# Retention and MLP on one core: one group of units fewer turned on TensorE, another order of loads, other rules of joining visits

## The chip, the cores and the metric

The kernel runs on one core of one Trainium2 chip. The time is the device time of one execution in microseconds; the median of several executions is given.

## The reference

The inputs are q, k and v of 8 batches x 8 heads x 576 positions x 64, and two weights of an MLP, 512 x 2048 and 2048 x 512, all fp32.

```python
scores = scale * np.matmul(q, k.transpose(0, 1, 3, 2))
gamma = 1.0 - 2.0 ** (-5.0 - np.arange(H, dtype=np.float32))
rel = pos[:, None] - pos[None, :]
Dmat = np.where(rel >= 0, gamma[:, None, None] ** rel[None, :, :], 0.0)
attn_out = np.matmul(scores * Dmat[None, :, :, :], v)
...
x = np.ascontiguousarray(attn_out.transpose(0, 2, 1, 3)).reshape(B * S, H * D)
h = x @ w_in
g = 0.5 * h * (1.0 + erf(h * inv_sqrt2))
out = g @ w_out
```

So it is a causal attention with a decay in place of the softmax, and behind it an MLP with an exact GELU over 4608 tokens.

## The kernel before

**Units and groups.** The attention is cut into 36 units of 128 tokens with all 8 heads: for each pair of batches `bp` and chunk of positions `ci`, one unit for each batch `j`; the last chunk has 64 positions and holds both batches in one unit. Units 0 to 3 are the first chunks of batches 0 to 3 and are groups 0 to 3; after them a group is the two units of one `(bp, ci)`, so group 4 is units 4 and 5, group 5 units 6 and 7. There are 22 groups. Because the decay is a power, a chunk needs only its own keys (a masked product) and a state `u` of the chunks before it. Four units make a block of 512 tokens, x of that block, and the MLP runs over 9 blocks.

**Stages of a group.** Loads go through POOL's DMA queue and cast fp32 to bf16 on the way. `T`: q and k are turned (positions to the free axis). For groups 0 to 3 and for the `NPE` groups from 4 on (`BY_PE`) this is `turn`: 8 matmuls against an identity for q and 8 for k (line 528 calls the helper on line 454), and a copy out of PSUM by DVE or ACT, whichever is free sooner (`either`, lines 485 and 487). For the others (`BY_DVE`) it is `turn_dve`: q and k are loaded in another layout (line 346, runs of four positions), DVE transposes 32 x 32 blocks (line 548), and ACT takes q apart (`apart`, line 559). `S`: scores on TensorE, then the mask on DVE (line 612 or 617). `vh`: values scaled by the decay, on ACT, DVE or POOL (lines 634 and 638). `A`, a visit (`attend`): the products of scores and values, the new state, the product of q with the old state, and x out of PSUM by DVE (lines 785 and 789). `AA` is one visit for two groups. The state needs the keys in natural layout: for `BY_PE` groups that is the tile k was loaded in, for `BY_DVE` groups an extra tile `kn`, loaded by line 352.

**MLP.** The first product with w_in (`mlp1`, and `mlp1_fast` for the last three blocks), GELU on ACT, and the second product with w_out (`mlp2` for half of block 0, `mlp2_fast` for the rest). The fast forms use seven products in place of eight with sums made on DVE. `wi0` to `wi7` and `wo0` to `wo7` are 256 KB pieces of the two weights (lines 310 and 325), each needed by a part of the columns. `mlp1` of block 0 can start on a piece of w_in and one unit of x; `mlp2` of block 0 takes the pieces of w_out in order.

**What sets the order.** The instruction lists are written when the kernel is built, by a planner that keeps a clock for each engine (`T`), an estimate for each instruction and landing times for the loads. At each step it emits what its clock calls ready: attention first (A, U for a state, S, T), otherwise a step of the MLP. On the chip each engine then runs its list in order and waits on semaphores. A load is emitted from the list `ORDER` whenever POOL's clock is within 1.5 us of TensorE's; `q5` means q of unit 5, `n6` the keys of units 6 and 7 in natural layout, `io` and `dq` are small computations on POOL. Item `n` of a `BY_PE` group does nothing (line 329). After the list, later groups are loaded as buffers come free. While TensorE has nothing to do early on, the planner emits products of zeros (`warm`).

The constants in the diff are read in these lines:

```python
tied = 4 <= n < N_G - 1 and units[g[0]][1] == units[groups[n + 1][0]][1] and n >= VISIT and nB - 4 * b1 > LEAD
...
hold = both <= now + NEAR
...
if n < nT and n not in [x[0] for x in apart_due] and g[-1] // 4 <= tM1 + N_XB - 1 and nA + len(g) <= AHEAD + early + RATE * b1:
    return sg[n]["T"]
...
if T["dve"] <= now + (SB + JOIN_SB if after_a else SB) and nA - nB <= 2:
    acts.append((max(s_ready(JOIN if after_a else 0), fetch_at(64 if n >= 4 else 0), free_time(0, len(g))), "S"))
```

`nB` counts units attended, `nA` units whose scores are made, `b1` blocks through the first MLP product. A tied group waits for its partner if the partner is ready within `NEAR`. `SLACK`, `PER_G`, `PER_B` and `TURN0` rank DVE's side jobs, `SEM` is the planner's time for a semaphore, `STATE10` the earliest time of one state, and `MSK_AT` the time from which DVE may build the mask for groups 4 and later (`make_msk`, lines 213 and 215).

Of the kernel before, what the change touches and what calls it, by code (L numbers as in the profile page):

```python
# [17 lines left out]
def kernel(  # L18
# [48 lines left out]
    pair_of = {key: [units.index((*key, 0)), units.index((*key, 1))] for key in {x[:2] for x in units if x[2] is not None}}  # L67

    PLAIN = 4
    NPE = 2  # L70
    FAST1 = (5, 6, 7, 8)[PLAIN // 4:]
    FAST2 = tuple(range(1, N_BLK))
    BY_PE = range(4, 4 + NPE)
    BY_DVE = range(4 + NPE, N_G)
    raw = range(4)
# [6 lines left out]
    N_VH = 4  # L82
    VH_ACT = [4, 22, 1]
    N_XB = 4
    AHEAD = 35
    RATE = 0.4
    STORE_AT = 62.0
    CROWD = 66.0
    STATE10 = 28.0
    HOT = 8.0  # L90
    FETCH = 5.0
    ARRIVE = 5.4
    WARM_TO = 24.0
    JOIN = 1
    JOIN_SB = 0.0
    VISIT = 8
    LEAD = -3.0
    NEAR = 3.2
    SLACK, SB, PER_G, PER_B, TURN0 = 1.2, 2.0, 8.0, 20.0, 0.0
    FINE = 0.38  # L100
    FPOOL = 0.6
    N_V = 6
    N_WARM = 10
    MSK_AT = -58.0
    HK = N_DF // 2

    const = ctx.enter_context(tc.tile_pool(name="const", bufs=1))
# [11 lines left out]
    mode = ["full"]  # L119
    DRAIN = 0.25  # L120
    port_end = [0.0]
    SEM = 0.12
    OVER = {"dve": 0.06}

    pool_runs = []
# [96 lines left out]

    later = [(7.3, "act", 1.4, warm_gelu), (MSK_AT, "dve", 0.8, make_msk)]
    T["act"], T["dve"], T["pool"] = 2.6, 2.9, 1.25
# [39 lines left out]
    def all_loaded():  # L264
        return not ORDER and next_load[0] >= N_G

# [38 lines left out]
    def load(what, i):  # L305
# [56 lines left out]
        for jj in (j,) if j is not None else range(2):  # L362
# [3 lines left out]
            else:  # L366
# [6 lines left out]
    land["v", 0] = 6.2  # L373
    cast_due = {("q", 0): (loaded[0][0][0], first["q32"]), ("k", 0): (loaded[0][0][1], first["k32"])}
    cast_due["v", 0] = (loaded[0][1], first["first_v"])
    ORDER = ("wi4 io wo2 q2 q1 k1 k2 wi5 wi3 n4 v1 wi1 v2 wi0 wi2 k3 q3 v3 wi7 dq2 wi6 wo6 q4 wo4 q5 wo0 wo1 wo3 "
             "wo5 k5 wo7 q6 k4 k7 v4 q7 k6 q8 v6 q12 dq0 q9 v12 k9 k13 q10 n8 k11 k8 v8 dq3 k10 q11 v10 k12 n10 "
             "dq4 q13 n6 n12").split()

    def next_order():  # L380
        item = ORDER.pop(0)
        what = item.rstrip("0123456789")
        load(what, int(item[len(what):] or 0))
# [5 lines left out]
    def reload():  # L389
        if next_load[0] < N_G:  # L390
            g = groups[next_load[0]]
            ORDER.extend([f"{what}{i}" for what in "qk" for i in g] + [f"{what}{g[0]}" for what in ("vn" if len(g) > 1 else "v")])
            next_load[0] += 1
# [46 lines left out]
    def release(b, when):  # L440
        held.remove(b)
        free_at[b] = when
# [72 lines left out]
    def turn(n, jj):  # L515
# [15 lines left out]
        release(b, done + 0.05)  # L531
        sg[n]["T"] = max(sg[n].get("T", 0.0), done + SEM)

# [7 lines left out]
    def turn_dve(n, x):  # L541
# [6 lines left out]
        nc.vector.transpose(dst.rearrange("p (h b t) -> p h t b", h=HP, b=32), src)  # L548
        done = on("dve", 0.13 + m / 530, max(land["qk"[x], i] for i in groups[n])) + SEM
        if x == 0:  # L550
# [4 lines left out]
    def apart():  # L555
# [4 lines left out]
                       sg[n]["pairs"].rearrange("p h s -> p (h s)")[:, 0:2 * m].rearrange("p (n y) -> p y n", y=2))  # L560
        sg[n]["T"] = max(sg[n].get("T", 0.0), on("act", 0.15 + m / 580, ready) + SEM)

# [38 lines left out]
    def masked(i):  # L601
# [8 lines left out]
        if i in raw:  # L610
            for e in range(2):
                nc.vector.tensor_tensor(both[:, HP * e:HP * e + HP, :], t[:, e], near[e], op=ALU.mult)
                s["R"] = on("dve", 0.66, done) + SEM
                release(two[e], s["R"])
            return
        by = (msk2 if short else msk).unsqueeze(1).to_broadcast([128, 2, HP, w])
        nc.vector.tensor_tensor(both.rearrange("p (e h) s -> p e h s", e=2), t, by, op=ALU.mult)  # L617
        s["R"] = on("dve", 0.15 + H * w / 960, done) + SEM
        for b in two:
# [6 lines left out]
    def scaled_v(n, engine):  # L626
# [5 lines left out]
        if engine == "act":  # L632
            for h in range(H):
                nc.scalar.activation(vh[:, 0:m, h], src[:, :, h], AF.Copy, scale=dv[:, h, ci:ci + 1])  # L634
            done = on("act", 1.65 + 0.4 * m, ready) + SEM
        else:
# [7 lines left out]
    def out_pairs(n):  # L644
        return 2 if n >= 4 else 0
# [566 lines left out]
    def fire():  # L1212
        now = T["pe"]
        while ORDER and T["pool"] <= now + 1.5:
            next_order()
# [47 lines left out]
    def attend(*ns):  # L1263
        nonlocal nB
        two = out_banks(ns) if ns[0] >= 4 else ()
        for i in [i for n in ns for i in groups[n]]:
            inner(i)
            nB += 1
        while u_due and state_at(*u_due[0]) <= T["pe"] + 0.2 and not (u_due[0] == (1, 0) and T["pe"] <= STATE10):
            state(*u_due[0])  # L1270
# [13 lines left out]
    def s_ready(early=0):  # L1284
        n = group_of[nA]
        g = groups[n]
        if n < nT and n not in [x[0] for x in apart_due] and g[-1] // 4 <= tM1 + N_XB - 1 and nA + len(g) <= AHEAD + early + RATE * b1:
            return sg[n]["T"]
# [14 lines left out]
    while True:  # L1303
# [18 lines left out]
        if nB < nA:  # L1322
# [3 lines left out]
            ready = ready_for(n)  # L1326
            tied = 4 <= n < N_G - 1 and units[g[0]][1] == units[groups[n + 1][0]][1] and n >= VISIT and nB - 4 * b1 > LEAD
            if tied:
                both = 1e9
                if nA > groups[n + 1][-1] and one_piece(384 if len(g) > 1 else 192):  # L1330
                    both = max(ready, ready_for(n + 1))
                    acts.append((max(both, fetch_at(384 if len(g) > 1 else 192), free_time(len(g) > 1 and units[g[0]][1] < NCI - 1, out_pairs(n))), "AA"))
                hold = both <= now + NEAR
                alone = max(ready, free_time(n < 4, out_pairs(n)))
            else:
                acts.append((max(ready, fetch_at(192 if n >= 4 else 0), free_time(n < 4, out_pairs(n))), "A"))
        for key in u_due[:1]:
            if key != (1, 0) or now > STATE10:
                acts.append((state_at(*key), "U"))
        if nA < N_U:  # L1340
            n = group_of[nA]
            g = groups[n]
            if T["dve"] <= now + (SB + JOIN_SB if after_a else SB) and nA - nB <= 2:
                acts.append((max(s_ready(JOIN if after_a else 0), fetch_at(64 if n >= 4 else 0), free_time(0, len(g))), "S"))
        if nT < 4 + NPE and nT <= group_of[min(nA, N_U - 1)] + 3 and (nT < 4 or not half or ring_free("tk")):
            keys = [("qk"[half], i) for i in groups[nT]]
# [102 lines left out]
```

## Time and profile before

| | us |
|---|---|
| median of 3 runs (lowest, highest) | 288.04 (287.86, 289.65) |
| the profiled execution | 288.46 |
| its span, first to last instruction | 286.7 |
| TensorE busy in the span | 277.8 (97%) |
| DVE, ACT, POOL busy | 229.7, 176.7, 141.0 |
| moved by DMA | 31.97 MB |

The profile is of one execution. Its lines name an engine, the line of the kernel, the operation and its tiles (out<-in), how many and how long. TensorE's matmuls overlap one another, so a run of them is longer than the distance to the next start, and distances between starts are the better measure. Line 450 is the helper that records all matmuls, line 454 the one for transposes.

### The profile page before, as it was taken

The numbers are of one execution on the slowest core, as the hardware profiler recorded it, in microseconds if no ns is written. First come the engines' busy times: TensorE is split into PE (matmuls) and PEld (weight loads), VectorE is DVE, ScalarE is ACT, GpSimd is POOL, SyncE is SP. The second block draws the span as 40 slices with busy tenths as digits, with TensorE's granted clock in tenths as the row PEclk, the third lists the DMA queues.
The fourth block names the chain that finished last, engine by engine and source line by source line (L and its number), as shares of the span: only waits on it lengthen the run. The fifth ranks groups of instructions, "written<-read, shape, count | busy, mean of one in ns | idle before, by whom it ended". The sixth has DMA issues, their size and how long they took to land.

```text
span 286.7 us, 9851 instructions
## 1 busy us (share of the span) xinstructions
PE 277.8 (97%) x4216; PEld 210.3 (73%) x4216; DVE 229.7 (80%) x387; ACT 176.7 (62%) x403; POOL 141.0 (49%) x213
## 2 busy tenths in 40 slices
PE   7889998999999999999999999999999999999994
PEld 2568766888864657756676676677888888888883
DVE  6754586767995699898978599969999999999861
ACT  7456425876888895688587766764555363655421
POOL 8976898799959977778665864000000000000000
PEclk9999999999999999999999999999999999999999
DMA  9999999999999999999999996302020201202014
GB/s 158 176 179 188 195 152 173 188 132 143 128 154 108 116 167 120 205 146 135 142 150 160 101 139 54 71 2 75 2 75 0 77 4 72 75 0 75 37 57 129
DMA packets 109276, 31.97 MB, mean 112 GB/s; under 512 B 85936, under 2 KB 104880, under 8 KB 109232
## 3 DMA queue, kind: packets, MB, share of 16 engines
q0 software_dynamic: 100528, 21.12, 83.8%
q1 hardware_dynamic: 6752, 9.37, 9.9%
q10 hardware_dynamic: 1952, 0.85, 1.3%
q8 instruction: 33, 0.54, 0.8%
q14 instruction: 11, 0.09, 0.1%
HBM read 42.99 MB, written 9.44 MB: 183 GB/s over the span
## 4 chain that ended last, share of the span: by engine, by line
PE 61%; DMA 22%; POOL 12%; issue 2%; ACT 1%; DVE 0%; POOLq 0%
PE psum L450 60%; DMA kn_ld<-in_k_dram 6%; DMA w_out<-in_moe_w_out_dram 6%; DMA q_ld<-in_q_dram 5%; POOL k_ld L346 3%; POOL q_ld L346 2%; DMA v_ld<-in_v_dram 2%; DMA early<-in_q_dram 2%; POOL v_ld L357 2%; DMA k_ld<-in_k_dram 1%; POOL dqT L320 1%; PE psum L454 1%; POOL kn_ld L352 1%; POOL w_in L310 1%; POOL k_ld L336 1%
## 5 line engine op out<-in xcount | busy, mean ns | idle before, releaser
L450 PE MATMUL psum<-x,w_in 128*128 128x256 bf16 (+2 forms) x792 | 117.8, 295 | 0.6 <-DMA w_in<-in_moe_w_in_dram 0.6
L450 PEld LDWEIGHTS <-w_in 128*128 128x128 bf16 x792 | 69.0, 98 | 29.1 <-DMA w_in<-in_moe_w_in_dram 1.2
L450 PEld LDWEIGHTS <-g_all 128*128 128x128 bf16 x576 | 55.5, 98 | 13.5 <-issue 0.3
L450 PE MATMUL psum<-w_out,g_all 128*128 128x256 bf16 (+1 forms) x440 | 57.9, 280 | 0.0
L346 POOL DMA_DIRECT2D k_ld<-in_k_dram x64 | 35.5, 577 | 23.8 <-DMA kn_ld<-in_k_dram 14.1
L816 ACT ACTIVATE g_all<-psum 128x512 bf16<-128x512 f32 x64 | 36.9, 592 | 16.4 <-PE psum L450 14.8
L450 PEld LDWEIGHTS <-s 128*128 128x128 bf16 x408 | 39.5, 98 | 7.6 <-issue 0.6
L634 ACT ACTIVATE vh<-v_ld,dv 128x128 bf16<-128x128 bf16 (+1 forms) x144 | 42.1, 378 | 0.0
L617 DVE TENSOR_TENSOR ret<-psum,msk 128x1024 bf16<-128x1024 f32 (+1 forms) x32 | 35.5, 1149 | 6.3 <-PE psum L450 6.2
L1030 ACT ACTIVATE g_all<-t 128x512 bf16<-128x512 f32 x36 | 22.6, 630 | 28.2 <-DVE t L1038 28.2
L487 ACT COPY t<-psum 128x256 f32<-128x256 f32 (+1 forms) x48 | 20.7, 433 | 29.7 <-PE psum L450 29.5
L346 POOL DMA_DIRECT2D q_ld<-in_q_dram x64 | 35.6, 583 | 1.9 <-DMA k_ld<-in_k_dram 1.0
L450 PE MATMUL psum<-wt,s 128*128 128x256 bf16 x272 | 33.5, 273 | 0.3 <-ACT t L487 0.3
L901 DVE TENSOR_TENSOR o_sb<-psum,t 128x256 f32<-128x256 f32 x51 | 21.4, 420 | 13.1 <-PE psum L450 7.2
L1038 DVE TENSOR_TENSOR t<-psum,t 128x512 f32<-128x512 f32 x36 | 24.6, 687 | 2.7 <-ACT t L487 1.1
L819 ACT ACTIVATE g_all<-psum 128x256 bf16<-128x256 f32 (+1 forms) x43 | 19.5, 488 | 11.2 <-PE psum L450 10.6
L485 DVE COPY t<-psum 128x512 f32<-128x512 f32 (+1 forms) x39 | 21.6, 564 | 0.4 <-PE psum L450 0.3
L450 PE MATMUL psum<-x,ws 128*128 128x256 bf16 x144 | 19.5, 273 | 0.0
L450 PE MATMUL psum<-wt,g_all 128*128 128x256 bf16 x136 | 17.5, 273 | 0.0
L450 PE MATMUL psum<-w_out,s 128*128 128x256 bf16 x136 | 17.5, 273 | 0.0
L357 POOL DMA_DIRECT2D v_ld<-in_v_dram x14 | 16.5, 1180 | 1.0 <-ACT g_all L816 0.7
L785 DVE TENSOR_TENSOR x<-psum,dqT 128x1024 bf16<-128x1024 f32 (+1 forms) x14 | 15.5, 1137 | 0.1
(100 smaller groups left out, 326.2 us busy)
## 6 DMA issues: line engine op xcount, KB each, us to landing
out_dram<-o_sb SPq DMA_DIRECT2D x31, 256.0 KB, 3.3
q_ld<-in_q_dram POOLq DMA_DIRECT2D x56, 64.0 KB, 5.5
k_ld<-in_k_dram POOLq DMA_DIRECT2D x56, 64.0 KB, 4.7
v_ld<-in_v_dram POOLq DMA_DIRECT2D x14, 256.0 KB, 5.3
kn_ld<-in_k_dram POOLq DMA_DIRECT2D x12, 256.0 KB, 6.8
w_in<-in_moe_w_in_dram POOLq DMA_DIRECT2D x8, 256.0 KB, 8.4
w_out<-in_moe_w_out_dram POOLq DMA_DIRECT2D x8, 256.0 KB, 7.1
q_ld<-in_q_dram POOLq DMA_DIRECT2D x16, 32.0 KB, 4.5
```

The lines of the kernel that those rows point to most:

```text
L346: nc.gpsimd.dma_start(qk["qk".index(what)][p0:p0 + 32, 0:HP * per].rearrange("p (h x) -> p h x", h=HP), {"q": q, "k": k}[what][2 * bp + jj ...
L357: nc.gpsimd.dma_start(v_ld.rearrange("p j h d -> p (j h) d"), v[2 * bp:2 * bp + 2, :, ci * C:ci * C + C, :].rearrange("b h s d -> s (b h) d"))
L450: nc.tensor.matmul(*a, **k)
L485: nc.vector.tensor_copy(dst, src)
L487: nc.scalar.copy(dst, src)
L617: nc.vector.tensor_tensor(both.rearrange("p (e h) s -> p e h s", e=2), t, by, op=ALU.mult)
L634: nc.scalar.activation(vh[:, 0:m, h], src[:, :, h], AF.Copy, scale=dv[:, h, ci:ci + 1])
L816: nc.scalar.activation(g_all[:, t % 2, :, m0, :], hT.rearrange("p n (a c) -> p (n a) c", a=2), AF.Gelu)
L819: nc.scalar.activation(g_of(t, 2 * lo // TOK)[:, m0:m0 + n, lo_:lo_ + hi - lo], hT, AF.Gelu)
L901: nc.vector.tensor_tensor(dst, src, f[key], op=ALU.add)
L1030: nc.scalar.activation(g_of(t, part)[:, m0:m0 + 2], src, AF.Gelu)
L1038: nc.vector.tensor_tensor(f[key], f["b"][1], f[key], op=ALU.add)
```

## The change

`NPE` goes from 2 to 1: group 5 (units 6 and 7) is turned by DVE and ACT instead of TensorE, its q and k are loaded by line 346 instead of 336, and `n6` becomes a real load. The list of loads has the same items in another order. The rules: a pair may be joined from group 6 on instead of 8, but only if the attention is 7 units ahead of the first MLP product instead of -3; the wait for a partner is 1.2 instead of 3.2 us; scores may run ahead of the MLP by 13 units plus 4 for each block (before 35 plus 0.4), with no extra unit behind a visit. The mask is built from 18 us on instead of at once, one state from 40 us instead of 28, and three weights of the planner differ.

```diff
-    NPE = 2
+    NPE = 1
...
-    AHEAD = 35
-    RATE = 0.4
+    AHEAD = 13
+    RATE = 4.0
...
-    STATE10 = 28.0
+    STATE10 = 40.0
...
-    JOIN = 1
+    JOIN = 0
...
-    VISIT = 8
-    LEAD = -3.0
-    NEAR = 3.2
-    SLACK, SB, PER_G, PER_B, TURN0 = 1.2, 2.0, 8.0, 20.0, 0.0
+    VISIT = 6
+    LEAD = 7.0
+    NEAR = 1.2
+    SLACK = 1.2
+    SB = 1.7
+    PER_G = 8.0
+    PER_B = 8.0
+    TURN0 = 0.0
...
-    MSK_AT = -58.0
+    MSK_AT = 18.0
...
-    SEM = 0.12
+    SEM = 0.15
...
-    ORDER = ("wi4 io wo2 q2 q1 k1 k2 wi5 wi3 n4 v1 wi1 v2 wi0 wi2 k3 q3 v3 wi7 dq2 wi6 wo6 q4 wo4 q5 wo0 wo1 wo3 "
-             "wo5 k5 wo7 q6 k4 k7 v4 q7 k6 q8 v6 q12 dq0 q9 v12 k9 k13 q10 n8 k11 k8 v8 dq3 k10 q11 v10 k12 n10 "
-             "dq4 q13 n6 n12").split()
+    ORDER = ("q1 io wi0 k1 k2 wi3 k3 v1 q2 q3 wo4 v2 wi5 k4 wi2 v3 wi7 wi6 k5 q4 wi1 q5 dq2 wo2 wi4 wo0 wo1 wo3 "
+             "wo5 wo6 q8 wo7 k9 v4 q6 q7 k7 v6 n6 n4 k6 dq3 q9 v8 v10 k8 q11 n12 q10 n8 n10 q12 k10 dq0 k11 q13 "
+             "k13 k12 dq4 v12").split()
```

## The prediction

> **What bounds the kernel now.** I read the page first, then a table of TensorE's time by stage, then its instructions in order of time, and last the load queue on GpSimd.
>
> ```profile
> span 286.7 us, 9851 instructions
> PE 277.8 (97%) x4216; PEld 210.3 (73%) x4216; DVE 229.7 (80%) x387; ACT 176.7 (62%) x403; POOL 141.0 (49%) x213
> ```
>
> ```profile
> 0.00:10.00 10.00, 7.83 (x49) 3.24 (x49) 7.35 (x35) 7.08 (x14) 8.88 (x17) 1.00 1.22 161
> 10.00:20.00 10.00, 8.74 (x164) 6.14 (x159) 6.92 (x13) 4.46 (x10) 8.17 (x10) 1.00 1.78 183
> ...
> 40.00:50.00 10.00, 8.87 (x202) 7.26 (x200) 7.10 (x11) 5.40 (x14) 8.96 (x13) 1.00 1.72 174
> 50.00:60.00 10.00, 10.00 (x205) 8.54 (x203) 6.40 (x7) 8.43 (x19) 8.27 (x13) 1.00 1.49 173
> 60.00:70.00 10.00, 10.00 (x205) 8.56 (x203) 7.16 (x9) 7.39 (x18) 10.00 (x16) 1.00 1.69 135
> 70.00:80.00 10.00, 10.00 (x205) 8.56 (x203) 9.97 (x16) 8.10 (x25) 9.05 (x15) 1.00 1.55 137
> ...
> 240.00:250.00 10.00, 10.00 (x94) 8.97 (x92) 9.15 (x19) 5.41 (x10) 0.00 (x0) 1.00 0.14 53
> ```
>
> The columns are the stretch, its length, then busy time (and count) of PE, PEld, DVE, ACT and POOL, the granted clock, the DMA share and GB/s. From 50 us TensorE stands busy throughout at clock 1.00, and late in the run 94 matmuls of 256 columns pass in 10 us, 106.4 ns each: nothing can be taken out there except work. What is open lies before 50 us: 2.17 us idle in the first ten, 1.26 in the next, 1.13 in 40 to 50. In that early part POOL, which issues nearly all loads, is 8 to 9 of 10 busy and the DMA share is at its highest, so the order of loads sets what TensorE may do; later the loads run under TensorE. Hence I cost the change as work or waiting taken off TensorE, and ask at each place whether a load takes the place of what is removed.
>
> **Group 5 (units 6 and 7) off TensorE.** Its turning is in this stretch of TensorE's timeline (start, length, instructions):
>
> ```profile
> 33.01 8.12 PE L450 MATMUL psum<-w_out,g_all 128*128 128x512 bf16 x40
> 40.97 0.61 PE L454 MATMUL psum<-ident,k_ld 128*128 128x128 bf16 x8
> ...
> 43.25 0.62 PE L450 MATMUL psum<-q_ld,kT 32*128 32x128 bf16 x32
> 43.81 1.05 PE L450 MATMUL psum<-wt,s 128*128 128x256 bf16 x8
> 45.94 0.61 PE L454 MATMUL psum<-ident,q_ld 128*128 128x128 bf16 x8 [1.08 <-DMA q_ld<-in_q_dram]
> 46.38 1.04 PE L450 MATMUL psum<-w_out,g_all 128*128 128x256 bf16 x8
> 47.47 0.61 PE L454 MATMUL psum<-ident,k_ld 128*128 128x128 bf16 x8
> 48.01 0.63 PE L450 MATMUL psum<-ret,vh 128*32 128x128 bf16 x32
> ...
> 51.59 3.67 PE L450 MATMUL psum<-x,w_in 128*128 128x256 bf16 x32
> ```
>
> The lengths overlap, so I take start to start: 45.94 to 46.38 is 0.44 us, 47.47 to 48.01 is 0.54. These 16 transposes go: -0.98 us. The wait of 1.08 us ahead of the first goes too, since the product at 46.38 needs nothing from that load: -1.08. Together -2.06 at most.
>
> What is late next is the visit at 48.01, which needs the scaled values of group 4, and behind it x for block 1's first product at 51.59:
>
> ```profile
> 43.63 2.44 ACT L634 ACTIVATE vh<-v_ld,dv 128x128 bf16<-128x128 bf16 x8
> ```
>
> Its values stand at 46.07. They cannot come sooner, because v4 is item 35 of the old list and 34 of the new, behind the same 16 weight loads. So the visit can move from 48.01 to 46.07 and block 1 from 51.59 to 49.65: 1.94 us. Between 48.01 and 51.59 group 5's scores also stood, and these now come later, since group 5 waits for its DVE turns; they are as long as group 4's at 43.25 (0.56 to the next start). Of 1.94 there remain 1.94 - 0.56 = 1.38. **I take -1.4**; the bounds are -2.06 and 0 (all of it turned into waiting for x).
>
> What replaces the 16 transposes, on the other engines:
>
> ```profile
> L548 DVE STREAM_TRANSPOSE kT<-k_ld x16: 403/1105/1169, 62.0 to 188.1; 128x512 f32<-128x512 f32 x12, 128x256 f32<-128x256 f32 x4
> ...
> L485 DVE COPY q_ld<-psum x2: 690/690/691, 31.9 to 46.6; 128x1024 bf16<-128x1024 bf16 x2
> ...
> L559 ACT COPY q_ld<-qT x16: 610/1037/1052, 55.8 to 190.9; 128x1024 bf16<-128x1024 bf16 x12, 128x512 bf16<-128x512 bf16 x4
> ```
>
> DVE gains two transposes of 1.1 us and loses the 0.69 copy; ACT gains 1.04 us and loses the copy of the keys (about 1 us). DVE is net +1.5 us, between 45 and 55 us, where it is 6.4 to 7.1 of 10 busy: covered, **0**. Without cover all 1.5 us would stand before group 5's scores and its x, for which block 1's second half waits; TensorE then has the first half (64 products, 6.9 us) to run, so it takes more than that to show. Bounds 0 to +1.5.
>
> The Trainium skill, "SBUF — State Buffer", section "Who interferes with whom", would speak against this part: DVE copies in a two-port mode lock GpSimd out of the ports that it writes descriptors through. If the transposes did that, two of 1.1 us could hold the load queue for 2.2 us. The first row below has 64 k_ld issues of 542 to 664 ns, over a time in which DVE made nearly all its transposes; by the rule the sum would be up to 2.2 us worse, by the row it is unchanged.
>
> **Loads.** Group 5's q and k change form (line 336 to line 346), and a key load in natural layout is added (n6, which did nothing before):
>
> ```profile
> L346 POOL DMA_DIRECT2D k_ld<-in_k_dram x64: 542/575/664, 49.6 to 173.2; - x64
> ...
> L352 POOL DMA_DIRECT2D kn_ld<-in_k_dram x12 | 14.2, 1180 | 0.0
> ...
> L336 POOL DMA_DIRECT2D k_ld<-in_k_dram x8 | 6.0, 761 | 1.5 <-DMA w_out<-in_moe_w_out_dram 1.4
> ```
>
> On POOL, eight issues of 0.76 become eight of 0.58, and one of 1.18 is added: -0.3 us. On the DMA engines 256 KB more at 137 GB/s are 1.9 us of the queue, and everything behind n6 can be that much later. TensorE is without idle from 50 to 80 us and has those 6.9 us of block 1 to run before group 5 is needed, so I take **0**; bounds 0 and +1.9.
>
> **The start.** The new list asks for q1 first and has units 1 to 3 complete (v3) as item 16 instead of 18, but spreads the w_in pieces: the last is item 25, not 21. The mask, built at once before, is held to 18 us:
>
> ```profile
> 7.25 0.40 PE L450 MATMUL psum<-qkT 64*128 64x128 bf16 x8 [0.30 <-DVE qkT L485]
> ```
>
> ```profile
> 7.11 0.47 DVE L213 TENSOR_SCALAR msk<-val 128x128 f32<-128x128 f32 x1
> 7.62 0.68 DVE L215 COPY msk<-msk 64x64 f32<-64x64 f32 x2
> 8.32 1.29 DVE L612 TENSOR_TENSOR ret<-psum,near 128x512 bf16<-128x512 f32 x2
> ```
>
> Unit 0's scores were done at 7.65 and DVE began on them at 8.32: without the mask unit 0's x is 0.67 us sooner. From 10 to 20 us TensorE also fills time with seven products of zeros (first and last below), 512 columns or 0.21 us each by the rate above, 1.5 us besides the 1.26 idle:
>
> ```profile
> 10.79 0.38 PE L450 MATMUL psum<-zeros 128*128 128x512 bf16 x1
> ...
> 15.22 0.38 PE L450 MATMUL psum<-zeros 128*128 128x512 bf16 x1
> ```
>
> So at most 2.8 us of real work could move in here. Against that stands the last w_in piece:
>
> ```profile
> 17.63 0.81 POOL L310 DMA_DIRECT2D w_in<-in_moe_w_in_dram  x1
> ...
> 31.13 0.73 POOL L325 DMA_DIRECT2D w_out<-in_moe_w_out_dram  x1
> ```
>
> ```profile
> DMA to landing us min/median/max: 6.1/8.4/9.6
> ```
>
> It was the 20th thing that POOL did from 1.25 us on, 0.86 us each; in the new list it is the 29th (q and k of units 4 and 5 are two issues each, n4 none), one of the nine cheap: some eight more, 24.5, landing at 32.9. Its products with four units are 32 of 128 columns, 0.053 each, 1.7 us: block 0's second MLP starts at 34.6 instead of 33.01. From there TensorE has 32 products of 512 and 56 of 256 columns (6.8 + 6.0 us), a visit (1.16, below) and group 4's scores and key turn (0.6 + 0.4): 15.0 us, done at 49.6, just when v4 lets block 1 begin (49.65). So a start late by 1.6 costs nothing, and what is won before 33 us mostly waits for v4. **I take -0.3**, half of the mask's 0.67; bounds -2.8 (all filler replaced) and +1.5 (third rival).
>
> **Joining.** A pair of groups is visited together if units attended minus 4 times the first MLP's progress exceeds LEAD, now 7, before -3.
>
> ```profile
> 67.60 0.63 PE L450 MATMUL psum<-ret,vh 128*32 128x128 bf16 x32
> ...
> 68.76 1.92 PE L450 MATMUL psum<-w_out,g_all 128*128 128x256 bf16 x16
> ...
> 81.19 1.89 PE L450 MATMUL psum<-x,w_in 128*128 128x512 bf16 x8
> ...
> 90.29 3.63 PE L450 MATMUL psum<-x,w_in 128*128 128x512 bf16 x16
> 93.85 1.08 PE L450 MATMUL psum<-ret,vh 128*32 128x128 bf16 x64
> ...
> 96.07 2.76 PE L450 MATMUL psum<-x,w_in 128*128 128x512 bf16 x12
> ```
>
> At 93.85 twelve units were attended, and 48 of block 2's 64 products (81.19 to 90.29, four runs) were done: 12 - 4 x 2.75 = 1. That passes -3 and not 7; so though VISIT falls to 6, I expect fewer joined visits. A single visit takes 67.60 to 68.76, 1.16 us; a joined one 93.85 to 96.07, 2.22: joining saves 0.10. I expect four pairs undone, since the attention's lead grows late: **+0.4**; bounds 0 and +0.8 (all eight pairs from group 6 on). JOIN, NEAR, SB, SEM, AHEAD, RATE and PER_B only shift the same instructions; with TensorE full after 50 us, 0 within 0.3, three joins more or fewer.
>
> **Sum.** -1.4 + 0 + 0 - 0.3 + 0.4 = -1.3. The profiled execution took 288.46 us, 286.7 of it span; it becomes 287.2. The three runs have a median of 288.04, 0.4 below it: 288.04 - 1.3 = **286.7**.
>
> **Rivals.**
> 1. *The start closes up.* With units 1 to 3 early TensorE does turns, scores and visits in place of zeros, and v4's values come as soon as the loads ahead of them thin out. Some 2 of the 2.8 us are won besides: 284.7. For it: 10 to 20 us is the emptiest stretch after the first. Against: the w_in pieces come later, and v4 stays behind the same weights.
> 2. *Nothing arrives.* All of the -1.4 turns into waiting for group 4's or 5's loads, the start gives -0.3, the visits cost 0.4: 288.1. For it: POOL is 8 to 9 of 10 busy through 40 to 60 us. Against: TensorE was 10.00 busy from 50 us.
> 3. *The last w_in piece decides* (slower). After 17.63 POOL issued more slowly, thirteen to 31.13, 1.04 us each. At that pace the piece is issued at 26.0, and with the longest landing, 9.6, it is there at 35.6; block 0's second MLP starts at 37.3, its 15.0 us end at 52.3 and block 1 begins there instead of 51.59, with group 5's scores (0.56) still to come: +1.3, and +0.4 for the visits: 289.7. From a start after about 35.6 the kernel is no longer faster. For it: nothing can run ahead of that piece but attention, which needs loads too. Against: v3 as item 16 leaves TensorE 24 of the 32 unit-and-piece products before that piece lands.
>
> **Chances.** Forecast 0.43, the first rival 0.22, the second 0.21, the third 0.14. A measurement of this kernel tells about 1% from no change, 285.2 to 290.9. Faster by over 1% holds the first rival's larger part and a little of the forecast: 0.21. Slower by over 1% is a third of the third rival and some of the second, with n6's 1.9 and DVE's 1.5 added: 0.13. The rest, 0.66, is within 1%. The forecast's own range is 285.3 (-2.06, the mask's whole 0.67, no pair undone) to 287.7 (half of -1.4, nothing from the start). The range for 8 in 10 takes in most of the rivals: 284.2 to 290.2.
>
> **What would show it.** Right: 16 matmuls on line 454 on q_ld and k_ld instead of 32, no wait of TensorE for q_ld near 45 us, kn_ld x13, block 1's first product at 49 to 50.5 us instead of 51.59, block 0's second MLP from 33 to 34.6, mostly ret,vh runs of 32 after 60 us, and 94 matmuls per 10 us late. Wrong: that MLP starting before 32 or after 35.6 us, idle of TensorE at block boundaries after 50 us, or a lower granted clock.

## The result: slower by half a per cent, and the profile after

The kernel after takes **289.32 us** (median of 20 runs, 288.55 to 291.11), the kernel before 288.04 in the same comparison (20 runs): a ratio of 1.0052, 95% interval 1.0039 to 1.0064 (the two medians alone give 1.0044). The forecast was 1.3 us less; it is 1.3 us more. Two further comparisons, each within its own group of runs, gave 1.0020 (0.9996 to 1.0044) and 1.0045 (1.0026 to 1.0063).

The profiled execution of after took 288.55 us, the shortest of its 20. The page's first lines:

```profile
span 286.8 us, 9761 instructions
PE 279.0 (97%) x4158; PEld 209.1 (73%) x4162; DVE 229.5 (80%) x384; ACT 180.3 (63%) x405; POOL 140.7 (49%) x214
```

The stages (stretch, length, busy time and count of PE, PEld, DVE, ACT, POOL, granted clock, DMA share, GB/s):

```profile
0.00:10.00 10.00, 7.11 (x34) 2.94 (x35) 6.19 (x33) 7.08 (x14) 8.87 (x16) 0.90 1.29 156
10.00:20.00 10.00, 9.77 (x172) 6.31 (x172) 7.10 (x14) 3.94 (x9) 7.90 (x11) 0.93 1.94 175
...
40.00:50.00 10.00, 9.23 (x158) 6.92 (x158) 9.85 (x16) 6.44 (x18) 9.07 (x13) 1.00 1.82 191
50.00:60.00 10.00, 10.00 (x204) 8.54 (x202) 7.18 (x9) 9.48 (x23) 8.05 (x11) 1.00 1.80 166
...
240.00:250.00 10.00, 10.00 (x94) 8.98 (x92) 7.89 (x14) 5.68 (x10) 0.00 (x0) 1.00 0.15 54
```

The end is as before: 94 matmuls in 10 us. TensorE looks busier from 10 to 20 us (9.77 for 8.74), but that is no gain: part of the time is at a lower clock, and nine products of zeros start in it where before has seven. From 40 to 50 us DVE is now full (9.85 for 7.10).

TensorE's timeline of after, from the turn of group 4 to group 5's visit (start, length, instructions, idle before them and what ended it). The lines of this kernel are shifted: in after the helper for all matmuls is line 454 and the one for transposes line 458 (in e9, e13 and e17 lines 452 and 456).

```profile
29.70 0.61 PE L458 MATMUL psum<-ident,k_ld 128*128 128x128 bf16 x8
...
31.57 0.62 PE L454 MATMUL psum<-q_ld,kT 32*128 32x128 bf16 x32
...
33.88 5.53 PE L454 MATMUL psum<-w_out,g_all 128*128 128x512 bf16 x23
39.34 0.42 PE L454 MATMUL psum<-vh,early 128*32 128x64 bf16 x32
...
40.92 2.77 PE L454 MATMUL psum<-w_out,g_all 128*128 128x512 bf16 x20 [0.20 <-DMA w_out<-in_moe_w_out_dram]
...
45.37 1.06 PE L454 MATMUL psum<-ret,vh 128*32 128x128 bf16 x32
...
48.46 1.03 PE L454 MATMUL psum<-wt,g_all 128*128 128x256 bf16 x8 [0.46 <-ACT t L491]
49.33 4.53 PE L454 MATMUL psum<-x,w_in 128*128 128x256 bf16 x40
53.80 0.62 PE L454 MATMUL psum<-q_ld,kT 32*128 32x128 bf16 x32
54.35 2.79 PE L454 MATMUL psum<-x,w_in 128*128 128x256 bf16 x24
56.98 1.04 PE L454 MATMUL psum<-w_out,s 128*128 128x256 bf16 x8
57.95 0.63 PE L454 MATMUL psum<-ret,vh 128*32 128x128 bf16 x32
```

Each step that was forecast is there: the second MLP starts at 33.88 (33 to 34.6 expected), group 5's turns and the wait of 1.08 us for q_ld are gone, block 1 begins at 49.33 (49 to 50.5 expected) instead of 51.59. The signs that were named for a right forecast came true, and the kernel is slower all the same. At 49.33 block 0 isn't finished: its last step, eight products on w_out and s, stands at 56.98, behind block 1's first half.

**Equal work.** Lists in which the same products stand in another order can be compared at points at which two traces have the same work behind them. There are two such points in before and in all five executions of after, with the same scores and visits done and the same columns multiplied (group 5's turns apart). At the first, point A, block 0 has only its last step left: 50.06 in before, and the start of block 1 in after. At the second, point B, block 2 begins: 81.19 in before, 80.75 in after's profile.

```profile
50.06 1.04 PE L450 MATMUL psum<-w_out,s 128*128 128x256 bf16 x8
```

```profile
80.75 4.48 PE L454 MATMUL psum<-x,w_in 128*128 128x512 bf16 x20
```

"Late" is the difference in us to the trace of before; the end is that of TensorE's last matmul (282.94 in before).

| execution of after | us | wait on w_out | block 1 begins | late at A | late at B | late at the end |
|---|---|---|---|---|---|---|
| the profile above | 288.55 | 0.20 (at 41 us) | 49.33 | -0.73 | -0.44 | +0.10 |
| e6 | 288.72 | 0.42 | 49.48 | -0.58 | -0.28 | +0.26 |
| e11 | 289.05 | 0.33 | 49.78 | -0.28 | 0.00 | +0.56 |
| e16 | 288.51 | 0.35 | 49.27 | -0.79 | -0.51 | +0.05 |
| e18 | 289.24 | 0.69 | 49.97 | -0.09 | +0.19 | +0.74 |

Two things follow. From A to the end each of the five loses the same 0.82 to 0.84 us against the trace of before: 0.28 to 0.30 up to B, and 0.54 to 0.55 behind it. Up to A each is ahead, by 0.1 to 0.8 us, and what differs between executions is made there. Before itself isn't quite as even: in its two other executions (e8, e12) the stretch from B to the end is 0.27 us shorter than in its first profile, which has one run of scores drawn out by that much at 151 us; against them after loses 0.82 behind B.

Where a trace has no such point (e1, e3, e7), work is compared as the sum of the products' columns at full rate, without zeros and transposes, which is a rougher measure.

### The profile page after: what moved, and what is told of

Read it like the earlier page. It is cut to its first block, busy times and chain, and to the rows that moved or that the text cites. A ratio compares the mean times of both kernels' runs of the same rounds, so it can differ in the third digit from the quotient of the medians.

```text
span 286.8 us, 9761 instructions
## 1 busy us (share of the span) xinstructions
PE 279.0 (97%) x4158; PEld 209.1 (73%) x4162; DVE 229.5 (80%) x384; ACT 180.3 (63%) x405; POOL 140.7 (49%) x214
## 4 chain that ended last, share of the span: by engine, by line
PE 81%; DMA 8%; POOL 6%; DVE 1%; ACT 1%; issue 1%; DVEq 0%; POOLq 0%; ACTq 0%
PE psum L454 81%; DMA w_out<-in_moe_w_out_dram 3%; DMA k_ld<-in_k_dram 3%; POOL early L372 3%; DMA v_ld<-in_v_dram 2%; POOL w_in L314 1%; POOL q_ld L340 1%; POOL w_out L329 1%; ACT vh L638 1%; POOL dqT L324 0%; DVE kT L552 0%; DVE x L793 0%; DVE u_acc L716 0%; DVE o_sb L905 0%; ACT t L491 0%
## 5 line engine op out<-in xcount | busy, mean ns | idle before, releaser
L454 PEld LDWEIGHTS <-w_in 128*128 128x128 bf16 x752 | 68.2, 98 | 26.8 <-DVE x L793 0.4
L454 PE MATMUL psum<-w_out,g_all 128*128 128x256 bf16 (+1 forms) x438 | 58.8, 280 | 0.3 <-DMA w_out<-in_moe_w_out_dram 0.2
L350 POOL DMA_DIRECT2D k_ld<-in_k_dram x68 | 37.6, 575 | 20.6 <-DMA kn_ld<-in_k_dram 7.1
L621 DVE TENSOR_TENSOR ret<-psum,msk 128x1024 bf16<-128x1024 f32 (+1 forms) x32 | 35.6, 1148 | 6.2 <-PE psum L454 6.1
L350 POOL DMA_DIRECT2D q_ld<-in_q_dram x68 | 37.6, 579 | 1.9 <-DMA kn_ld<-in_k_dram 1.0
L491 ACT COPY t<-psum 128x256 f32<-128x256 f32 (+1 forms) x51 | 21.9, 430 | 24.6 <-PE psum L454 23.9
L823 ACT ACTIVATE g_all<-psum 128x512 bf16<-128x512 f32 (+1 forms) x38 | 19.0, 528 | 7.8 <-PE psum L454 7.5
L489 DVE COPY t<-psum 128x512 f32<-128x512 f32 (+1 forms) x36 | 20.3, 576 | 0.2 <-PE psum L454 0.2
L552 DVE STREAM_TRANSPOSE kT<-k_ld 128x512 f32<-128x512 f32 (+1 forms) x17 | 16.0, 940 | 1.6 <-DMA k_ld<-in_k_dram 1.6
```

The lines of the kernel that those rows point to most:

```text
L350: nc.gpsimd.dma_start(qk["qk".index(what)][p0:p0 + 32, 0:HP * per].rearrange("p (h x) -> p h x", h=HP), {"q": q, "k": k}[what][2 * bp + jj ...
L454: nc.tensor.matmul(*a, **k)
L489: nc.vector.tensor_copy(dst, src)
L491: nc.scalar.copy(dst, src)
L823: nc.scalar.activation(g_of(t, 2 * lo // TOK)[:, m0:m0 + n, lo_:lo_ + hi - lo], hT, AF.Gelu)
```

## The experiments

Each run makes the change shown, in the kernel before or after, or repeats one of them. A time in us is a median, "ratio" the ratio to before in the same group of runs, with its 95% interval.

**e1: group 5 off TensorE, alone** (in before).

```diff
-    NPE = 2
+    NPE = 1
```

> The kernel before with one edit: NPE = 1 (group 5 turned by DVE and ACT, n6 becomes a load; list of loads and rules as before). Theory A (the removal gains 1 to 2 us on TensorE and the new order of loads and the undone joins give it back): 286.0 to 287.2 against 288.04, 16 transposes on q_ld and k_ld, no wait for q_ld near 45 us. Theory B (the removal itself costs, because n6 and the DVE turns make group 5 late): 288.5 or more, with TensorE waiting or short of work between 50 and 65 us.

Measured: 293.98, ratio 1.0198 (1.0169 to 1.0228). Up to 67 us the part does what it should: equal work is reached 1.5 to 2.0 us sooner from 49 us on, 1.97 at A and 1.53 at 67 us. TensorE's timeline of e1, and a line of DVE's:

```profile
45.59 1.08 PE L450 MATMUL psum<-ret,vh 128*32 128x128 bf16 x32
...
47.20 1.05 PE L450 MATMUL psum<-wt,g_all 128*128 128x256 bf16 x8
48.09 1.04 PE L450 MATMUL psum<-w_out,s 128*128 128x256 bf16 x8
49.42 1.92 PE L450 MATMUL psum<-x,w_in 128*128 128x256 bf16 x16 [0.30 <-DVE x L785]
```

```profile
46.63 1.09 DVE L548 STREAM_TRANSPOSE qT<-q_ld 128x512 f32<-128x512 f32 x1
```

Block 1 begins at 49.42, nearly when it does in after, and here the last step of block 0 is already done, at 48.09. Block 1 waits 0.30 us for x of group 4; DVE came to this visit's results only at 47.57, behind a transpose of group 5. The loss comes later, from 70 to 105 us and from 192 us on, as idle time of TensorE (5.3 us in all behind 67 us): n6 is next to last in this list, and the state of group 5 is made only at 74.7. So the time is that of Theory B, but TensorE doesn't wait for group 5 between 50 and 65 us.

**e7: the same, with n6 behind v6.**

```diff
-    NPE = 2
+    NPE = 1
...
-             "... q8 v6 q12 dq0 ... dq4 q13 n6 n12"
+             "... q8 v6 n6 q12 dq0 ... dq4 q13 n12"
```

> The kernel before with NPE = 1 and n6 moved to stand right behind v6 (it was next to last in the list, where it had no effect). If the late n6 is what cost the first of these experiments its lead of 1.5 us between 70 and 100 us: the lead stays until 100 us, and the run is 2 us or more faster than that experiment (292 or less; 286.5 if nothing else is lost). If the rules and the rest of the list do it: 293 to 294 again.

Measured: 293.37, ratio 1.0188 (1.0163 to 1.0212). Ahead by about 1.4 us at 62 us as e1, it loses less up to block 2 (which begins at 82.91, in e1 at 84.59), and at the end the trace is as late as that of e1 (5.6 us for 5.2). n6 alone isn't what spoils it.

**e10: e7, with the first fast products of the last blocks held until all units are attended.**

```diff
+        if nB < N_U and name == "1":
+            return 1e9
```

> The kernel before with NPE = 1 and n6 behind v6, and one line more: no fast step of the first MLP product starts before the last visit is done. In the run without that line the last visit came at 250 us, and TensorE lost 3.9 us between 192 and 275 us. If the late visit causes that: the visit comes near 205 us, and the run is 2.5 to 4 us faster than 293.4. If the loss there has another cause: 293 again.

Measured: 292.73, ratio 1.0164 (1.0119 to 1.0209). The last visit moved from 250.1 us in e7 to 203.0, and the run is 0.6 us faster and not 2.5 to 4; TensorE still ends 4.5 us late (e7: 5.6). So the late last visit is at most a small part of that loss; why the old rules don't suit a list without group 5's turns stays open.

**e3: the new list alone** (in before, group 5 on TensorE).

```diff
-    ORDER = ("wi4 io wo2 q2 q1 k1 ...
+    ORDER = ("q1 io wi0 k1 k2 wi3 ...
```

> The kernel before with the new list of loads alone (n6 stays without effect). Theory A (the new order starves the first MLP of block 0 before 30 us): 0.5 to 1.5 us slower than before, less MLP work done at 20 us. If the order is neutral: within 0.3 us of before. Theory B expects no loss here.

Measured: 308.24, ratio 1.0678 (1.0632 to 1.0724). It is 0.87 us late at A and 1.3 to 1.5 by equal work from 53 to 75 us, so the new list costs something early, as Theory A had it. It loses 15 us more by the end, most of it from 200 to 255 us; where that comes from stays open.

**e9: after with the first 25 items of the old list.**

```diff
-    ORDER = ("q1 io wi0 ... wo2 wi4 wo0 wo1 wo3 "
+    ORDER = ("wi4 io wo2 q2 ... q4 wo4 q5 k4 k5 wo0 wo1 wo3 wo5 "
```

> The changed kernel with the first 25 items of its list of loads put back as before (all of w_in and units 1 to 3), the rest in the new order. If the new start costs 0.9 to 1.3 us that are never won back: TensorE is ahead of the changed kernel by 0.9 to 1.3 us from 20 to 65 us, and ahead of the kernel before by 1.5 to 2. If the start is hidden behind v4, as the prediction had it: level with the changed kernel from 50 us on. The end depends on what the planner makes of the rest: 288.0 to 288.5 if nothing else moves.

Measured: 295.18, ratio 1.0238 (1.0205 to 1.0271). A miss: with the old head block 0's second MLP starts at 35.05, with the same work behind it as in after (33.64 to 33.95), so it isn't ahead but 1.1 to 1.4 us later. Where most of the time went after that, on TensorE and on ACT:

```profile
47.69 1.05 PE L452 MATMUL psum<-w_out,g_all 128*128 128x256 bf16 x8
52.78 1.03 PE L452 MATMUL psum<-wt,g_all 128*128 128x256 bf16 x8 [4.05 <-ACT t L489]
```

```profile
50.03 2.44 ACT L636 ACTIVATE vh<-v_ld,dv 128x128 bf16<-128x128 bf16 x8 [3.13 <-DMA v_ld<-in_v_dram]
52.38 0.35 ACT L489 COPY t<-psum 128x256 f32<-128x256 f32 x1
```

In ACT's list the values of group 5 now stand ahead of a copy that TensorE needs; ACT waits 3.13 us for v6, and TensorE 4.05 behind it. This one wait is longer than the whole difference between before and after.

**e2: the joining rules alone** (in before).

```diff
-    JOIN = 1
+    JOIN = 0
...
-    VISIT = 8
-    LEAD = -3.0
-    NEAR = 3.2
+    VISIT = 6
+    LEAD = 7.0
+    NEAR = 1.2
```

> The kernel before with the four constants of joining alone (JOIN 0, VISIT 6, LEAD 7, NEAR 1.2). Theory A (each joined visit undone costs about 0.1 us): one joined visit of 64 left instead of four, 0.3 to 0.7 us slower than before. Theory C (joining is where the whole loss lies): 1.3 us slower or more. No loss: joins cost nothing.

Measured: 289.74, ratio 1.0052 (1.0028 to 1.0076), so by the times what Theory C asked. After 60 us its timeline has 14 visits of attention on TensorE and before has 9. Its trace is 0.93 us ahead at A, 0.94 at B, and 0.50 late at the end: 1.4 us for five visits more. Why it is ahead at all: group 5 is still turned on TensorE, but the wait of 1.08 us for its q_ld is gone; no idle time stands at this line:

```profile
45.22 0.61 PE L454 MATMUL psum<-ident,q_ld 128*128 128x128 bf16 x8
```

So the new rules alone take away the wait that the prediction credited to group 5's turn.

**e5: no pair joined** (in before).

```diff
-    VISIT = 8
+    VISIT = 99
```

> The kernel before with VISIT = 99: no pair is joined, so four joined visits and one joined pair of short groups are taken apart; loads, turns and start stay as before. If a joined visit saves 0.33 us (counted from the end of the product ahead of it): 1.3 to 2 us slower than before, from 90 us on. If it saves 0.10 us (counted from its own first matmul, as in the prediction): 0.4 to 0.5 us.

Measured: 289.64, ratio 1.0056 (1.0035 to 1.0078). By the medians that is 1.6 us slower than before, as a saving of 0.33 asked. In the trace there are 16 visits, and 1.2 us are lost from B to the end for seven visits more.

**e4: after with the joining rules of before** (the diff of e2 the other way round, in after).

> The changed kernel with the four constants of joining as before (JOIN 1, VISIT 8, LEAD -3, NEAR 3.2). Theory A: 0.3 to 0.7 us faster than the changed kernel's 289.32, so 288.6 to 289.0. Theory C: 288.0 or less. If joining costs nothing: 289.3.

Measured: 294.09, ratio 1.0201 (1.0164 to 1.0238). None of the three. It has four visits of a joined pair and is slower by 5 us, which are lost between 94 and 128 us, 2.22 of them in one stop:

```profile
105.00 0.50 PE L454 MATMUL psum<-wt,s 128*128 128x256 bf16 x3
107.72 0.72 PE L454 MATMUL psum<-wt,s 128*128 128x256 bf16 x5 [2.22 <-issue]
```

So the old rules don't suit the new list, and this run says nothing of the price of a join.

**e6, e11, e16, e18: after again; e8, e12: before again.** No edit.

> The changed kernel once more, for a second profile, since its first profiled execution is the fastest of its runs. If the loss is the start and the joins alone, TensorE's work is behind the kernel before by the same amounts in both profiles up to 50 us, and the span is near 287.5 us. If something else makes its usual execution longer, a stretch appears that the first profile does not have.

> The kernel before, unchanged, for a second profile: how much TensorE's progress moves from one execution to another. Expected within 0.4 us of the first profile at every point; if it moves by 1 us, differences of that size between single profiles show nothing.

> The changed kernel a third time, for another profile. Two of its profiles show TensorE ending at 282.8 and 282.9 us and no idle of TensorE put down to its own instruction supply; its usual execution is 0.6 us longer. If the supply of instructions is what varies, a slower execution shows an idle stretch of 0.5 to 1.2 us inside a run of equal products.

> The kernel before a third time. Its second profile has TensorE idle for 1.05 us at 58.5 us inside a run of equal products, the first has not. Expected: one of the two forms, and a time that goes with it (288.0 to 288.5 without, 289.2 with).

> The kernel after, unchanged, on the chip of the three others, to compare them with: 289.3, and 1.005 times the kernel before.

> The kernel after, unchanged, beside the run before this one: 289.1 to 289.3, and a stop of 0.2 to 1.2 us on w_out at 34 to 36 us in its trace.

Measured: after as in the table; e16 and e18 were also timed, 289.07 and 289.26. Before took 289.28 in e8 and 287.85 in e12. The trace of e8 is that of before up to 58 us (0.12 us sooner at A), and then has a stop of 1.05 us inside one run of products, which stays to the end:

```profile
56.23 2.25 PE L450 MATMUL psum<-x,w_in 128*128 128x256 bf16 x19
59.53 2.67 PE L450 MATMUL psum<-x,w_in 128*128 128x256 bf16 x23 [1.05 <-issue]
```

So e8 misses its 0.4 us, by a stop that can be seen as one; apart from it the three traces of before lie within 0.35 us of each other at A. A figure from a single profile (e2, e5, e13 to e15) is no surer than that, but the length of a stretch repeats better. After has no such stop behind 51 us in its five traces: e11, which looked for one, differs by its waits ahead of 50 us. e18 came out as expected.

**e13: after, with q1 sixth in the list.**

```diff
-    ORDER = ("q1 io wi0 k1 k2 wi3 k3 ...
+    ORDER = ("io wi0 k1 k2 wi3 q1 k3 ...
```

> The kernel after with one item of its list moved: q1 from first place to sixth, behind wi3, as it stands behind the first weights in the old list; all else as in after. Unit 0's scores then stand ahead of unit 1's turn on TensorE, as in the kernel before. Theory (what the start loses is owed later): up to 40 us TensorE is 0.8 to 1.1 us ahead of after at equal work, and at least half of this is still there from 50 us to the end: about 0.5 to 1 us less time than after, 288.3 to 288.8. Rival (the prediction's: a late start is made up while block 1 waits for v4): ahead up to 40 us, level with after from 50 us on, same time as after, 289.3.

Measured: 289.38, 0.3 more than e16 beside it (-0.3 to +0.6). A miss for the theory: unit 0's x comes sooner, but those of units 1 and 2 come later, and block 0's second MLP starts at 33.76 with the same work done, as in after (33.64 to 33.95). It then waits 1.03 us for w_out and is 0.92 us behind the best execution of after (e16) at A, and 0.86 at the end: nothing is made up on the way. So the first place of q1 isn't where after loses.

**e14: after, with the mask at once.**

```diff
-    MSK_AT = 18.0
+    MSK_AT = -58.0
```

> The kernel after with MSK_AT back at -58, so that DVE builds the mask at once. The instruction list of TensorE is that of after but for one product of zeros. The prediction took 0.3 us for the mask's delay (half of 0.67). Theory (the delay of the mask brings nothing, since after waits for unit 1's query in that stretch): same time as after within 0.3 us, 289.3. Rival (the prediction's): 0.3 to 0.7 us more than after, 289.6 to 290.0.

Measured: 289.80, 0.7 more than e16 (0.3 to 1.4). By the times the rival was right and the later mask is a gain. The trace says how little of it arrives: the second MLP starts at 34.21 with the same work done, 0.3 to 0.6 us later than in after, but then waits only 0.09 us for w_out, and at A it stands as after's five do in the mean (-0.47 for -0.49). It also has a stop of 0.60 us at 159.73 that has nothing to do with a mask. So the gain is shown by the times alone, with a size of 0.3 to 1.4.

**e15: after, with one pair joined more.**

```diff
-    LEAD = 7.0
+    LEAD = 6.0
```

> The kernel after with LEAD 6 instead of 7: the list has one joined visit more (11 single and 2 joined visits of pairs instead of 13 and 1). Theory (each stretch of attention fewer saves 0.25 to 0.33): 0.3 us less than after, 289.0. Rival (a join saves 0.10, as the prediction had it): 289.2. Other rival: the joined visit delays x of the next block, as in the run of after with the old joining rules, and it is slower by 1 us or more.

Measured: 289.30, 0.2 more than e16 (-0.2 to +0.8): inconclusive by the times. In its trace the part from B to the end costs 0.42 instead of 0.55: 0.13 for the one join.

**e17: after, with two pieces of w_out exchanged.**

```diff
-             "... k3 v1 q2 q3 wo4 v2 ... wo0 wo1 wo3 wo5 ..."
+             "... k3 v1 q2 q3 wo3 v2 ... wo0 wo1 wo4 wo5 ..."
```

> The kernel after with the items wo3 and wo4 of its list in each other's place: the piece of w_out that block 0's second MLP needs fourth comes as item 11 instead of 28, the one that it needs fifth takes the late place. TensorE's instruction list is the same as that of after. Theory (the late start goes on as a wait for a piece of w_out, 0.2 to 1.2 us in the traces so far, and is not made up): no stop of TensorE on w_out after its first four products of that MLP, at equal work 0.3 to 1.0 us ahead of after from 37 us on and to the end; 288.4 to 288.9. Rival (another wait takes its place before block 1 begins, values or the sums of w_out on DVE): ahead at 37 us, level from 50 us on, 289.1 to 289.3.

Measured: 289.30, as e18 beside it (-0.5 to +0.3). I had moved the wrong piece. Four products belong to one piece (two rows of blocks for two tiles of tokens), so after the first four TensorE waits for wo1, the second, and wo1 kept its place. The wait is still there; three executions of this list of TensorE:

```profile
35.02 4.48 PE L454 MATMUL psum<-w_out,g_all 128*128 128x512 bf16 x20 [0.35 <-DMA w_out<-in_moe_w_out_dram]
```

```profile
35.67 4.48 PE L454 MATMUL psum<-w_out,g_all 128*128 128x512 bf16 x20 [0.69 <-DMA w_out<-in_moe_w_out_dram]
```

```profile
36.07 4.48 PE L452 MATMUL psum<-w_out,g_all 128*128 128x512 bf16 x20 [1.18 <-DMA w_out<-in_moe_w_out_dram]
```

They are e16, e18 and e17, profiled at 288.51, 289.24 and 289.57 us. The run doesn't decide what its theory asked, as the wait wasn't taken away; but it is a sixth execution of the same list of TensorE, and from A on it too loses 0.82.

## Why the prediction was wrong

In the traces the change is the sum of these terms, each against the first trace of before:

| term | predicted | measured in traces |
|---|---|---|
| group 5 off TensorE | -1.4 | -1.53 (e1, at 67 us) |
| the start, up to A | -0.3 | +1.04 (five executions of after at A, mean -0.49, less e1's -1.53) |
| between A and B, where no join differs | 0, within 0.3 | +0.28 |
| joining, behind B | +0.4 | +0.55 |
| sum | -1.3 | +0.34 |

The split between the first two is one way of telling it. Alone in before, the parts stand at A at -1.97 (e1), -0.93 (e2) and +0.87 (e3), and these don't add up to -0.49: e1 and e2 take away the same wait for q_ld.

**Group 5: right in size, nearly right in mechanism.** Its turns and the wait went, and e1 lies between the forecast and its bound. Two things were not foreseen: the wait goes by the rules alone as well (e2), and DVE's part isn't wholly covered, since in e1 block 1 waits 0.30 us for an x that stood behind a transpose. The rule of the Trainium skill on shared ports ("SBUF — State Buffer", "Who interferes with whom") was said to change nothing for the load queue. After has more DVE transposes than before, and the median of its key loads is 568 ns for 575; the trace doesn't show the rule's effect on them:

```profile
L350 POOL DMA_DIRECT2D k_ld<-in_k_dram x68: 542/568/717, 33.5 to 171.0; - x68
```

**The start: the step that failed.** The prediction counted 15.0 us of TensorE work without any wait from the start of block 0's second MLP, "done at 49.6, just when v4 lets block 1 begin", hence "a start late by 1.6 costs nothing". Both times came true, 33.88 and 49.33, but by luck: the work between them is another, it contains waits, and block 1 doesn't wait for v4.

First, the start is hardly late. When the second MLP starts, after has already turned group 4's keys and made its scores (0.45 and 0.55 us from start to start) and has one state still to make (0.35), so of the 0.63 to 0.94 us by which the five executions start behind before, 0.65 are other work: 0.16 us late in the mean.

Second, the loss is made inside the second MLP, by three waits of TensorE, none of which e1 has:

- For pieces of w_out: 0.20 to 0.69 us, 0.40 in the mean, in four of five for the second piece, wo1. I followed the last piece of w_in, but the pieces of w_out come behind it, the last one landing at 40.9 us instead of 38.3 in before. Among the traces of before only e8 shows such a wait, of 0.08.
- For a sum of w_out that DVE makes: 0.32 to 0.34 us in four of the five, none in the first. The eight sums end at 41.5 us in before and at 46.6 to 48.0 in after.
- For a copy that ACT makes out of PSUM between two steps of the MLP: 0.46 us in all five. In before and e1 a visit stands between the two steps, in e1 from 45.59 to 47.20, and covers the copy; in after the visit stands ahead of both.

The last two in e16 (the first is the line at 35.02 above), with DVE's and POOL's work ahead of them:

```profile
47.34 0.60 PE L454 MATMUL psum<-w_out,g_all 128*128 128x256 bf16 x4 [0.32 <-DVE w_out L874]
48.40 1.03 PE L454 MATMUL psum<-wt,g_all 128*128 128x256 bf16 x8 [0.46 <-ACT t L491]
```

```profile
45.41 1.88 DVE L874 TENSOR_TENSOR w_out<-w_out 128x1024 bf16<-128x1024 bf16 x1
```

```profile
45.68 1.05 POOL L324 TENSOR_TENSOR dqT<-dqT,step 128x512 f32<-128x512 f32 x1
```

Together they are 1.12 us in the mean, for a term that is 1.34 off. As gains they don't add up: in e16 x is out at 49.02, so without the copy's wait alone block 1 could begin some 0.2 us sooner and not 0.46. Values of v4 aren't what block 1 stands behind in after: in the first profile they are through ACT by 45.92, x is out by 48.56, and block 1 begins at 49.33, right behind the last products ahead of it. In e1, which has none of the three waits, the work to the end of block 0 still takes 16.1 us and not 15.0, with 0.30 idle behind it; so the count was short as well, and there was little time in which a late start could hide. That a late start does hide in part is seen in e14, but behind w_out and not behind v4.

The three waits are read from traces. No run took one of them away: e17 moved another piece. e13 shows that q1 isn't the cause. Which change of the list or of the rules makes each wait wasn't tried by itself.

**Joining: right in sign, and not far off in size.** The number was right: of before's five joined visits with 64 products one is left (at 178.88), so four pairs are undone, and a short pair (108.82 in before) besides. Measured behind B, the five visits more cost 0.55 us against the first trace of before and 0.82 against the two others, inside the bounds of 0 to +0.8 or at their edge: 0.11 to 0.16 for each. In the single traces of the others, e15's one join is 0.13, e5's seven visits are 0.17 each, and e2's five 0.29 each, with another order of scores too. The forecast's 0.10 lies below all of these. One reason is that the prediction priced a visit from its first product to the next run, and a switch also costs between the last product ahead and the visit's first. In before the run ahead of the single visit is

```profile
64.00 3.67 PE L450 MATMUL psum<-x,w_in 128*128 128x256 bf16 x32
```

32 products of 0.1064, to 67.41; so the visit costs 68.76 - 67.41 = 1.35 and not 1.16. The joined one, behind 16 products of 0.2133 from 90.29, costs 96.07 - 93.70 = 2.37. By that estimate a join saves 0.33, which is more than these traces show. For after a part of the gap can be read: before's list has a stop behind B that after's hasn't, and it sets off part of the price.

```profile
123.09 1.03 PE L450 MATMUL psum<-wt,s 128*128 128x256 bf16 x8 [0.33 <-ACT t L487]
```

**Between A and B.** No pair is joined here in either kernel, and after loses 0.28 us, most of it in two places of block 1: a visit that takes 0.11 us longer (68.65 in after) and 0.14 ahead of the scores at 72.80. The prediction allowed 0.3 for the other rules.

**From the traces to the medians.** +0.34 is the mean difference of the profiled executions. Before's own profiled execution was 0.42 above its median, which the prediction took off; after's five lie 0.5 below its median (288.81 in the mean for 289.32), which nobody could know. 0.34 + 0.42 + 0.51 = 1.27. Why the unprofiled executions of after are longer than the profiled ones isn't shown (in e2 and e5 they are too, by 0.8 and 0.7); a longer wait for w_out, as e17's 1.18, would do it, but those executions have no trace.

**The rivals.** The third, the slower one, came nearest in time (289.7), but not by its route. It let the last w_in piece hold up block 0's second MLP until 37.3, and asked for a start after 35.6; the piece was issued at 26.14, as it said, but landed at 31.3 and not 35.6, the MLP started at 33.88, and it was w_out, DVE's sums and ACT's copy that TensorE waited for. "A lower granted clock" was listed as proof against the forecast, and there was one:

```profile
8.00:9.00 1.00, 1.00 (x12) 0.50 (x11) 0.68 (x2) 0.99 (x2) 1.00 (x2) 0.53 2.43 156
9.00:10.00 1.00, 1.00 (x4) 0.43 (x3) 1.00 (x3) 0.14 (x1) 1.00 (x2) 0.50 1.88 180
...
11.00:12.00 1.00, 0.84 (x20) 0.48 (x19) 0.20 (x1) 0.59 (x1) 0.98 (x3) 0.77 2.42 155
```

It follows an idle of 0.97 us at 6.7 to 7.7 and falls in large part on products of zeros. It isn't the cause: two of the five executions, e16 and e18, keep a clock of 1.00 there, and they start the second MLP at 33.64 and 33.95, the three others at 33.69 to 33.94.

**What stays open:** which of the changes makes each of the three waits, and what the kernel would gain without them; why the change's parts are so much worse alone (+6 for e1, +20 for e3) than together, beyond the waits named; and the 0.5 us between after's profiled and other executions. No version here beat the kernel before: every kernel tried has a ratio above 1, though e16's interval reaches below it.

## What to carry to other kernels

A delay is hidden only if the engine would have stood idle at the meeting point: before a term is set to nothing, find that idle time in a row, and follow each thing that the stretch needs (the weights, the sums made from them, the copies out of PSUM) to the moment when it is there. Compare lists at points where the same work is done, turns included, and not by when a block begins, because a planner that reorders can begin a block in time and leave other work behind. And price a switch between kinds of work from the end of the run ahead to the start of the run behind, then check it against a run.

## What was not expected of the hardware

TensorE can stop in the middle of a run of like products for which the profile shows nothing missing: 1.05 us in one of three traces of the kernel before, 2.22 us in e4, 0.60 us in e14, each put down to "issue". Such a stop is as large as the effect studied, and the first isn't in every execution of the same list.

A sum on DVE took up to three times as long while POOL computed beside it. In all five executions of after, the last sum of w_out overlaps POOL's computation of dq and takes 1.27 to 2.11 us; the seven ahead of it, and all eight in before, stand clear of it and take 0.68 to 0.69. That the one holds up the other is inferred from the overlap; no run was made to move it.

A granted clock of half for some 3 us between 8 and 12 us left no mark on the time. And two executions of one list can differ by 0.3 us by the landing of a single 256 KB piece (a wait of 0.35 us in e16, 0.69 in e18), while the 230 us behind point A repeat within 0.02.
